# Attention plus token MLP on one core: the opening of the kernel is reordered (zero matmuls first, a long GpSimd memset cut up and put later, a query copy moved into the exponential stream)

## Chip, cores, metric

One core of a Trainium2 chip runs one program. The metric is the device time of one launch in microseconds (us); lower is better. Engines are named as in the profile: PE (TensorE, matmul), PEld (its weight loads), DVE (VectorE), ACT (ScalarE), POOL (GpSimd), SP (SyncE, which issues most DMAs).

## What is computed

The input `x` has 2048 rows (tokens) of 512. The output is `x + A(xn) + B(xn)` with `xn = layernorm(x)`. Cut to what matters:

```python
def A(x):                                   # 32 heads of width 16
    q, k, v = split_heads(x @ wqkv)
    p = softmax(q @ k.T * 16**-0.5)         # 2048 x 2048 for each head
    return merge_heads(p @ v) @ wo

def B(x):                                   # MLP across the tokens
    h = layernorm(x)
    u = gelu(h.T @ w1 + b1)                 # 1376 hidden
    return (u @ w2 + b2).T
```

All inputs and the output are bf16. The softmax is the bulk of it: 32 x 2048 x 2048 exponentials.

## The kernel before

**Tiling.** The tokens are cut in 16 tiles `t` of 128 rows. Queries are taken in 4 blocks of 512 (`qb`) and heads in 8 groups `G` of four, which gives 32 blocks `b`. A block goes through 16 key tiles `kt`; for each, two pairs of score matmuls (`score_mm`, L665: keys as weights, 512 queries moving, one pair for two heads) each fill two PSUM banks, 128x1024. So there are 32 x 16 x 2 = 1024 score pairs. One ACT instruction (`a_exp`, L742) takes the exponential of a whole pair into one of ten `pT` buffers. For some key tiles DVE takes ACT's place with an exponential made of integer and bf16 steps (`d_bits`, `d_chain`, L945 to L985: two reads of 1024 columns out of PSUM and four passes over 2048 columns in SBUF for each key tile). Four PV matmuls (`pv_round`, L766) then add the key tile to bank 6; a tile that went through DVE needs three such rounds.

**Order.** Every engine runs its own queue in order. The queues are written by a planner (`Dispatch`), which simulates the engines with estimated costs (`EST`) and at each simulated moment gives a free engine the ready step of the best priority. Steps become ready by planned times (`at`, `free_at`) and by `prog["p"]`, the number of key tiles scored so far in the plan, to which each score pair adds a half. What the planner writes is a fixed order; at run time only semaphores hold an instruction back. `Sched.add` finds the waits from the keys that each step reads and writes. Two engines that read the same PSUM bank are made to wait for each other as well (the `k[0] == "bank"` lines, L205 to L208). The planner's clock starts at `EST["start"]`.

**The prologue**, before the planned part, is written by hand (`pro_stage`, L601 to L627). `x` is loaded by SP in six DMAs (tiles 0, 1, 2-3, 4-7, 8-11, 12-15), `wqkv` by ACT in six. For a tile, DVE takes statistics (L497, L499), POOL makes the reciprocal deviation with two small instructions (L501, L503), DVE normalises (L512), PE transposes (L523) into a bank that ACT copies out to `xnT` (L518), and PE projects keys (L536), queries (L570) and values (L548) of the first four tiles for the first head group. The key projections of successive tiles use the same bank 6, so each waits until the last one's keys were copied out, on DVE for even tiles and on ACT for odd ones (`kt_tile_evac`). Statistics run to tile 5 here. At the end `qt0_evac` (L575) turns the queries of block 0 and 1, which stand in bank 7 (`EX_BANK`), into `QT`: ACT writes `QT[0]` (L576), DVE writes `QT[2]` (L578), ACT writes an unmasked copy `qst` (L580), and four SP DMAs spread `qst` into `QT[1]` and `QT[3]`, which block 1 needs. All three engine instructions read bank 7.

**The tile loop.** Key tiles 4 to 15 are made while block 0 is being scored (`tile_job`, L1294): for each tile statistics, normalise, transpose, copy, key and value projection, two copies out. DVE does all copies here.

**What POOL does at the start.** `ident` (identity for the transposes), `mhalf`, `zero`, `qmask`, then one memset of `QT[1..7]`, 128 x 3584 (L442), and only then the first L501. `clear_images` (L445) sends the zeroed `QT[4..7]` to a DRAM image, to which later queries are written. `keep_warm` (L1070) inserts pairs of matmuls with zero weights (L1077) where the planner counts too little PE work.

Of the kernel before, what the change touches and what calls it, by code (L numbers as in the profile page):

```python
# [31 lines left out]
NDB = 3  # L32
NPRE = 4
NQS = 4
NW1 = 2
# [13 lines left out]
QSCALE = 0.25 * LOG2E * 128.0  # L49
# [7 lines left out]
EST = dict(  # L57
    start=15.5, pe_switch=0.105, mm512=0.215, mm128=0.065, pe_lat=0.13,
    exp=0.924, exp_lat=1.45, tanh=0.75, act_lat=0.55,
# [15 lines left out]
class Dispatch:  # L75
# [17 lines left out]
    def done(self, *names):  # L93
        t = self.t
        at = self.at
        for n in names:
            if at.get(n, 1e9) > t:
                return False
        return True
# [212 lines left out]
def bass_parallel_sum__softmax_full_mha__mixer_token_mlp__prompt_kernel(  # L312
# [18 lines left out]
    with ExitStack() as es:  # L331
# [19 lines left out]
        qmask = sb("qmask", [128, 2], F32)  # L351
# [3 lines left out]
        QT = sb("QT", [128, 2 * NQS, 512], BF16)  # L355
# [26 lines left out]
        ident = sb("ident", [128, 128], BF16)  # L382
# [26 lines left out]
        def bank(i):  # L409
            return ps[:, i * 512:(i + 1) * 512]  # L410
# [11 lines left out]

        sc.add("pool", lambda e: e.memset(ident[:], 0.0), writes=[("ident",)])
        sc.add("pool", lambda e: e.affine_select(ident[:], ident[:], [[-1, 128]], ALU.not_equal, 1.0,
                                                 base=0, channel_multiplier=1),
               reads=[("ident",)], writes=[("ident",)])
        sc.add("pool", lambda e: e.memset(mhalf[:], -0.5), writes=[("mhalf",)])
        sc.add("pool", lambda e: e.memset(zero[:], 0.0), writes=[("zero",)])
        sc.add("dve", lambda e: e.memset(b1c_bf[:], 0.0), writes=[("b1c",)])
# [4 lines left out]
        sc.add("dve", lambda e: e.memset(v17_main[:, :, 16:17], 1.0), writes=[("Vone",)])  # L434
        sc.add("pool", lambda e: e.memset(qmask[:], 0.0), writes=[("qmask",)])
        for r in range(4):
            sc.add("pool", lambda e, r=r: e.memset(qmask[32 * r:32 * r + 16, r % 2:r % 2 + 1], QSCALE),
                   reads=[("qmask",)], writes=[("qmask",)])
        def qt_at(b, v):
            return 4 * (b // 2 % 2) + 2 * v + b % 2  # L440

        sc.add("pool", lambda e: e.memset(QT[:, 1:2 * NQS, :], 0.0), reads=[("qmask",)],  # L442
               writes=[("QT", q) for q in range(1, 2 * NQS)])

# [130 lines left out]
        def qt0_evac():  # L575
            sc.add("act", lambda e: e.activation(QT[:, 0, :], bank(EX_BANK), ACTF.Identity, scale=qmask[:, 0:1]),  # L576
                   reads=[("bank", EX_BANK), ("qmask",)], writes=[("QT", 0)])
            sc.add("dve", lambda e: e.tensor_scalar(QT[:, 2, :], bank(EX_BANK), qmask[:, 1:2], None, ALU.mult),  # L578
                   reads=[("bank", EX_BANK), ("qmask",)], writes=[("QT", 2)])
            sc.add("act", lambda e: e.activation(qst[:, :], bank(EX_BANK), ACTF.Identity, scale=QSCALE),  # L580
                   reads=[("bank", EX_BANK)], writes=[("qst",)])
            for r in range(4):
                q = 32 * r + 16
                dma("sp", QT[q:q + 16, 1 + 2 * (r % 2), :], qst[q:q + 16, :], reads=[("qst",), ("QT", 1 + 2 * (r % 2))],
                    writes=[("QT1", r)], name="qt_spread")
# [45 lines left out]
        done = dp.done  # L631
        free_at = {("pair", 0): 0.0, ("pair", 1): 0.0, ("pair", 2): None, "b4": 0.0, "b5": 0.0, "ex": 0.0, "pv": 0.0}

# [8 lines left out]
        at[("QT", 0)] = dp.t  # L642
        at[("QT", 1)] = dp.t + 4.0

# [696 lines left out]

        def clear_job():
            def go():
                clear_images()
                dp.use("sp", 2 * EST["sp"])
            yield ("sp", 0.2, lambda: prog["p"] > 2, go)

        dp.spawn(clear_job())
        for t in range(NPRE, NT):
# [150 lines left out]
```

## Time and profile before

| | us |
|---|---|
| median of 3 runs | 796.83 (796.32, 796.83, 798.67) |
| profiled execution, its time | 797.49 |
| its span, first to last instruction | 795.7 |
| ACT busy | 765.9 (96%) |
| PE busy | 723.8 (91%) |
| DVE busy | 714.1 (90%) |
| POOL busy | 73.0 (9%) |
| first exponential starts at | 16.49 |

How to read it: the span is what the profile covers, and 1.8 us of the execution's time lie outside it. Busy shares are averages over the whole span, so the opening, in which ACT, PE and DVE all wait for input, counts little in them. An instruction's row in the timeline gives its start, its duration (or that of several merged, with their number) and in brackets how long its engine was idle before it and what ended that. "Mean ns of one" of an exponential (1131) is longer than the distance between two of them, because they overlap at the ends; 756.5 us of busy time for 816 of them give 0.927 us each.

### The profile page before, as it was taken

How to read it: one execution, taken by the hardware profiler on the slowest of the kernel's cores; microseconds unless marked ns; L12 is line 12 of the kernel's file. 1: busy time of each engine (PE TensorE's matmuls, PEld its weight loads, DVE VectorE, ACT ScalarE, POOL GpSimd, SP SyncE). 2: the span in 40 equal slices, each digit the busy share in tenths (PEclk: the TensorE clock that was granted, in tenths of full speed). 3: DMA queues.
4: the chain of work that ended last, by engine and by line, in shares of the span. 5: the costliest groups of instructions: out<-in, count | busy, mean ns of one | idle time of the engine just before them, and what ended most of it. 6: DMA issues, size and time to landing. Idle time of an engine off the chain costs nothing.

```text
span 795.7 us, 14239 instructions
## 1 busy us (share of the span) xinstructions
PE 723.8 (91%) x5928; PEld 212.0 (27%) x5928; DVE 714.1 (90%) x948; ACT 765.9 (96%) x838; POOL 73.0 (9%) x110
## 2 busy tenths in 40 slices
PE   5999998999999899999899989999999999989885
PEld 3433332322222222222222222222222222222221
DVE  6888988999999799999999989998999999998888
ACT  4999999999999999999999999999999999999994
POOL 5233000000000010000000000000000000000000
PEclk9999999999999999999999999999999999999998
DMA  7402010102112122120302212112131112111001
GB/s 187 110 12 70 16 51 15 38 15 74 45 41 67 39 50 68 41 57 15 96 20 56 72 35 79 36 35 79 42 96 33 50 47 82 45 48 49 16 5 40
DMA packets 85184, 41.28 MB, mean 52 GB/s; under 512 B 61184, under 2 KB 81152, under 8 KB 85120
## 3 DMA queue, kind: packets, MB, share of 16 engines
q1 hardware_dynamic: 81952, 38.80, 18.3%
q10 hardware_dynamic: 3168, 1.57, 0.7%
q8 instruction: 46, 0.75, 0.4%
q14 instruction: 18, 0.15, 0.1%
HBM read 33.69 MB, written 5.37 MB: 49 GB/s over the span
## 4 chain that ended last, share of the span: by engine, by line
ACT 71%; PE 17%; DVE 9%; DMA 1%; issue 1%; POOL 0%; SPq 0%; ACTq 0%; DVEq 0%
ACT pT L742 71%; PE ps L665 7%; PE ps L766 5%; DVE xreg L945 3%; DVE big L979 1%; PE ps L1245 1%; PE ps L1174 1%; DMA xreg<-in_A_x_dram 1%; PE ps L1088 1%; DVE xreg L985 1%; DVE stats L497 0%; PE ps L1077 0%; DVE denb L1435 0%; DVE dmore L972 0%; ACT ga_sb L1203 0%
## 5 line engine op out<-in xcount | busy, mean ns | idle before, releaser
L742 ACT ACTIVATE pT<-ps 128x1024 bf16<-128x1024 f32 x816 | 756.5, 1131 | 8.2 <-PE ps L665 5.9
L665 PE MATMUL ps<-QT,KT 64*128 64x512 bf16 x2048 | 361.1, 385 | 52.7 <-ACT pT L742 30.7
L945 DVE TENSOR_SCALAR xreg<-ps 128x1024 int16<-128x1024 f32 x208 | 254.4, 1223 | 58.0 <-PE ps L665 53.6
L665 PEld LDWEIGHTS ps<-QT,KT 64*128 64x128 bf16 x2048 | 88.8, 93 | 338.9 <-ACT pT L742 219.8
L766 PE MATMUL ps<-pT,V 128*32 128x512 bf16 x1632 | 152.6, 388 | 1.2 <-ACT pT L742 0.9
L979 DVE TENSOR_TENSOR big<-xreg,big 128x2048 bf16<-128x2048 bf16 x104 | 128.2, 1233 | 0.0
L985 DVE TENSOR_SCALAR xreg<-xreg 128x2048 int16<-128x2048 int16 x104 | 73.2, 703 | 1.6
L965 DVE TENSOR_SCALAR big<-xreg 128x2048 int16<-128x2048 int16 x104 | 71.0, 683 | 0.1
L766 PEld LDWEIGHTS ps<-pT,V 128*32 128x32 bf16 x1632 | 37.6, 94 | 91.3 <-issue 84.6
L1245 PE MATMUL ps<-gT,w2blk 128*128 128x512 bf16 (+1 forms) x176 | 54.5, 385 | 0.0
L1174 PE MATMUL ps<-big,w1blk 128*128 128x512 bf16 (+1 forms) x176 | 52.9, 385 | 0.0
L895 POOL TENSOR_TENSOR oTe<-OT,denb 128x512 bf16<-128x512 f32 x15 | 20.7, 1380 | 337.6 <-DVE big L979 107.9
L766 PE MATMUL ps<-big,V 128*32 128x512 bf16 x556 | 48.2, 380 | 0.1
L766 PE MATMUL ps<-xreg,VS 128*32 128x512 bf16 x416 | 40.4, 379 | 0.2 <-DVE xreg L985 0.2
L895 POOL TENSOR_TENSOR oT<-OT,denb 128x512 bf16<-128x512 f32 x12 | 15.9, 1326 | 240.0 <-DMA denb<-den_scr 140.9
L972 DVE TENSOR_SCALAR xreg<-xreg 128x2048 int16<-128x2048 int16 x35 | 25.4, 725 | 0.0
L548 PE MATMUL ps<-wqkv_sb,xnT 128*128 128x128 bf16 x256 | 24.4, 225 | 0.1
L972 DVE TENSOR_SCALAR dmore<-xreg 128x2048 int16<-128x2048 int16 x34 | 24.4, 718 | 0.0
L972 DVE TENSOR_SCALAR big<-xreg 128x2048 int16<-128x2048 int16 x35 | 23.9, 683 | 0.0
L1077 PE MATMUL ps<-xnT,zero 128*128 128x512 bf16 x72 | 21.4, 384 | 0.4 <-ACT KT L518 0.2
L855 DVE COPY OT<-ps 128x512 f32<-128x512 f32 x31 | 21.2, 683 | 0.3 <-PE ps L766 0.2
L503 POOL TENSOR_TENSOR mv<-mv,mhalf 128x1 f32<-128x1 f32 x32 | 18.8, 586 | 2.7
(79 smaller groups left out, 373.0 us busy)
## 6 DMA issues: line engine op xcount, KB each, us to landing
denb<-den_scr SPq DMA_DIRECT2D x31, 256.0 KB
QT<-q_img SPq DMA_DIRECT2D x15, 512.0 KB
w1blk<-in_B_w_dram SPq DMA_DIRECT2D x10, 512.0 KB
w2blk<-in_B_w_dram SPq DMA_DIRECT2D x16, 320.0 KB
w1blk<-in_A_x_dram SPq DMA_DIRECT2D x16, 128.0 KB
out_dram<-osb SPq DMA_DIRECT2D x16, 128.0 KB, 1.7
q_img<-qst SPq DMA_DIRECT2D x30, 64.0 KB
xreg<-in_A_x_dram SPq DMA_DIRECT2D x3, 512.0 KB, 9.1
```

Of the source, the lines that this page charges most:

```text
L548: sc.add("pe", lambda e, ct=ct: e.matmul(bank(bk)[:, 128 * j:128 * (j + 1)], lhsT=xnT[:, ct, 128 * t:128 * (t + 1)], rhs=wqkv_sb[:, ct, 2 ...
L665: sc.add("pe", lambda e: e.matmul(bank(bk), lhsT=KT[64 * (r // 2):64 * (r // 2) + 64, T, 128 * kt:128 * (kt + 1)], rhs=QT[64 * (r // 2):64 ...
L742: sc.add("act", lambda e: e.activation(pT[:, buf, :], ps[:, s_ * 1024:(s_ + 1) * 1024], ACTF.Exp, scale=EXP_SCALE), reads=[("bank", 2 * s_ ...
L766: sc.add("pe", lambda e, r=r, lhs=lhs, rhs=rhs: e.matmul(bank(PV_BANK)[32 * r:32 * r + 32, :], lhsT=lhs, rhs=rhs, start=first, stop=last, ...
L895: sc.add("pool", lambda e: e.tensor_tensor(dst, OT32[:, eb, :], denb[:, :], ALU.mult), reads=[("OT32", eb), ("denb",)], writes=keys, extra ...
L945: sc.add("dve", lambda e: e.tensor_scalar(bv_i[:, i, 1024 * hf:1024 * (hf + 1)], ps[:, s_ * 1024:(s_ + 1) * 1024], EXP_BIAS, 0.0, ALU.add, ...
L965: sc.add("dve", lambda e: e.tensor_scalar(ge_i[:, i, :], bv_i[:, i, :], 0x7F, 0x3F00, ALU.bitwise_and, ALU.bitwise_or), reads=[("bD", i)], ...
L972: sc.add("dve", lambda e: e.tensor_scalar(vp_i(i), bv_i[:, i, :], 0x7F80, None, ALU.bitwise_and), reads=[("bD", i)], writes=[("vD", i)] + ...
L979: sc.add("dve", lambda e: e.tensor_tensor(ge_f[:, i, :], bv_f[:, i, :], ge_f[:, i, :], ALU.mult), reads=[("bD", i), ("eD", i)], writes=[(" ...
L985: sc.add("dve", lambda e: e.tensor_scalar(bv_i[:, i, :], bv_i[:, i, :], LIN_S, None, ALU.add), reads=[("bD", i)], writes=[("bD", i)])
L1174: mms = [lambda st=st: sc.add("pe", lambda e: e.matmul(bank(EX_BANK)[0:m, :], lhsT=w1blk[:, slot, st, 0:m], rhs=h_sb[:, st, :], start=(st ...
L1245: mms.append(lambda ft=ft, m=m: sc.add("pe", lambda e: e.matmul(bank(EX_BANK), lhsT=w2blk[0:m, slot, ft, :], rhs=gT[0:m, ft, :], start=(ft ...
```

## The change

Four edits in the opening, and what they need in the planner.

1. `zero` is now set first on POOL, and `NWARM = 9` matmuls of zeros by zeros, 128x512 into bank 4, stand at the head of PE's queue. `ident` follows `zero`.
2. `qmask` (five small memsets) moves from POOL to DVE, behind the memset of `V17` and ahead of the first statistics.
3. The memset of `QT[1..7]` becomes six memsets of 128x512 (`QT[2]`, which DVE writes in full, is left out), planned by `clear_job` on POOL once `prog["p"]` is above 0.5, 1.0, ... 3.0; `clear_images` follows them.
4. ACT's copy to `qst` and its four DMAs leave the prologue. `qst0_job` plans the copy at the front of ACT's queue once more than two score pairs have been fed, and the DMAs once the copy and the memsets of `QT[1]` and `QT[3]` are planned to be over. Bank 7 counts as taken until then.
5. `EST["start"]` is 12.0 for 15.5.

```diff
+NWARM = 9
-    start=15.5, pe_switch=0.105, mm512=0.215, mm128=0.065, pe_lat=0.13,
+    start=12.0, pe_switch=0.105, mm512=0.215, mm128=0.065, pe_lat=0.13,
...
-        sc.add("pool", lambda e: e.memset(ident[:], 0.0), writes=[("ident",)])
+        sc.add("pool", lambda e: e.memset(zero[:], 0.0), writes=[("zero",)])
+        for _ in range(NWARM):
+            sc.add("pe", lambda e: e.matmul(
+                bank(4), lhsT=zero[:, :], rhs=zero[:, :].unsqueeze(1).broadcast_to([128, 4, 128]), start=True, stop=True),
+                reads=[("zero",)], writes=[("bank", 4)])
+        sc.add("pool", lambda e: e.memset(ident[:], 0.0), reads=[("zero",)], writes=[("ident",)])
...
-        sc.add("pool", lambda e: e.memset(zero[:], 0.0), writes=[("zero",)])
...
-        sc.add("pool", lambda e: e.memset(qmask[:], 0.0), writes=[("qmask",)])
+        sc.add("dve", lambda e: e.memset(qmask[:], 0.0), writes=[("qmask",)])
         for r in range(4):
-            sc.add("pool", lambda e, r=r: e.memset(qmask[32 * r:32 * r + 16, r % 2:r % 2 + 1], QSCALE),
+            sc.add("dve", lambda e, r=r: e.memset(qmask[32 * r:32 * r + 16, r % 2:r % 2 + 1], QSCALE),
...
-        sc.add("pool", lambda e: e.memset(QT[:, 1:2 * NQS, :], 0.0), reads=[("qmask",)],
-               writes=[("QT", q) for q in range(1, 2 * NQS)])
+        def clear_qt(q):
+            sc.add("pool", lambda e: e.memset(QT[:, q, :], 0.0), writes=[("QT", q)])
...
+        def qst0():
             sc.add("act", lambda e: e.activation(qst[:, :], bank(EX_BANK), ACTF.Identity, scale=QSCALE),
                    reads=[("bank", EX_BANK)], writes=[("qst",)])
+
+        def qst0_spread():
             for r in range(4):
...
-        free_at = {("pair", 0): 0.0, ("pair", 1): 0.0, ("pair", 2): None, "b4": 0.0, "b5": 0.0, "ex": 0.0, "pv": 0.0}
+        free_at = {("pair", 0): 0.0, ("pair", 1): 0.0, ("pair", 2): None, "b4": 0.0, "b5": 0.0, "ex": None, "pv": 0.0}
...
-        at[("QT", 1)] = dp.t + 4.0
...
         def clear_job():
+            for k, q in enumerate((1, 3, 4, 5, 6, 7)):
+                def go(q=q):
+                    clear_qt(q)
+                    dp.use("pool", 0.5)
+                    if q == 3:
+                        at[("QT13",)] = dp.t + 0.6
+                yield ("pool", 0.6, lambda k=k: prog["p"] > 0.5 + 0.5 * k, go)
+
             def go():
                 clear_images()
                 dp.use("sp", 2 * EST["sp"])
-            yield ("sp", 0.2, lambda: prog["p"] > 2, go)
-
+            yield ("sp", 0.2, lambda: True, go)
+
+        def qst0_job():
+            def go():
+                qst0()
+                free_at["ex"] = dp.use("act", 0.6) + 0.2
+                at[("qst0",)] = free_at["ex"]
+            yield ("act", 0.0, lambda: a_cur["n"] > 2, go)
+
+            def go():
+                qst0_spread()
+                at[("QT", 1)] = dp.use("sp", 4 * EST["sp"]) + EST["dma"]
+            yield ("sp", 0.1, lambda: done(("qst0",), ("QT13",)), go)
+
+        dp.spawn(qst0_job())
         dp.spawn(clear_job())
```

What the compiled queues show of it: on ACT the `qst` copy now stands behind the second exponential. On POOL the first of the six memsets stands behind L501/L503 of tile 6, four behind those of tile 8, the last behind those of tile 9; none of them waits for a semaphore. The planned order differs from there on in many places: up to the 668th of 1024 score pairs the queues differ, and behind it they are equal but for the buffer numbers of DVE's key tiles. In all there are 814 exponentials on ACT for 816, 105 key tiles on DVE for 104, 76 zero-weight filler matmuls (L1077) for 72, and the nine new ones.

## The prediction

> **What bounds the kernel now.** I read the groups first. ACT's exponentials are busy 756.5 us of a 795.7 us span and were kept waiting 8.2 us in all.
>
> ```profile
> L742 ACT ACTIVATE pT<-ps 128x1024 bf16<-128x1024 f32 x816 | 756.5, 1131 | 8.2 <-PE ps L665 5.9
> ```
>
> So the end is: when the exponentials start (16.49), plus 816 x 0.927 = 756.5, plus some 8 us for the tanh instructions between them, plus the waits, plus the tail. A change in the opening counts only if the stream starts earlier and is not held up again, or if the planner gives ACT fewer exponentials.
>
> Then the chain of work that ended last, cut to the first 11 us (start, length, what):
>
> ```profile
> 2.12 6.91 DMA xreg<-in_A_x_dram
> 9.03 0.02 issue
> 9.05 0.71 DVE stats L497
> ...
> 9.96 0.30 DVE big L512
> 10.26 0.21 DVE KT L519
> ...
> 10.52 0.61 PE ps L536 x4
> ```
>
> The first ten us are set by a transfer: `x` tiles 4 to 7 land at 9.03, DVE's statistics of tile 4 wait for them, and behind these stand the normalise of tile 3 and the copy of tile 0's keys, for which PE waits until 10.52. Nothing ahead of 9.03 on DVE is on the path.
>
> Then the timeline of the opening:
>
> ```profile
> 2.34 3.09 POOL L442 MEMSET QT<- 128x3584 bf16 x1
> ...
> 6.30 0.41 DVE L512 TENSOR_SCALAR big<-xreg,mv 128x512 bf16<-128x512 bf16 x1 [1.32 <-POOL mv L503]
> ...
> 12.34 0.41 DVE L512 TENSOR_SCALAR big<-xreg,mv 128x512 bf16<-128x512 bf16 x1
> ...
> 13.05 0.63 PE L548 MATMUL ps<-wqkv_sb,xnT 128*128 128x128 bf16 x4
> ...
> 14.05 0.39 PE L548 MATMUL ps<-wqkv_sb,xnT 128*128 128x128 bf16 x4
> ...
> 15.84 0.60 ACT L580 ACTIVATE qst<-ps 128x512 bf16<-128x512 f32 x1 [0.90 <-DVE QT L578]
> ```
>
> POOL's memset does hold tile 0's normalise up by 1.32 us. PE is slow until about 13.6 (four matmuls start 0.43 apart) and then twice as fast (0.22). And `qst` waits 0.90 us for DVE while ACT could exponentiate.
>
> Last the tile loop (timeline, 16 to 36 us):
>
> ```profile
> 18.91 0.69 POOL L503 TENSOR_TENSOR mv<-mv,mhalf 128x1 f32<-128x1 f32 x1
> ...
> 28.11 1.94 ACT L742 ACTIVATE pT<-ps 128x1024 bf16<-128x1024 f32 x2 [0.26 <-PE ps L665]
> ...
> 30.34 1.94 ACT L742 ACTIVATE pT<-ps 128x1024 bf16<-128x1024 f32 x2 [0.29 <-PE ps L665]
> ```
>
> From 24 to 35 us a tile takes DVE 2.23 us (28.11 to 30.34), and two exponentials take ACT 1.94: DVE's loop, with POOL's L503 inside it, is the bound here, and ACT waits 0.26 to 0.29 for each tile. An earlier start of ACT alone is lost in that stretch.
>
> **Zero matmuls.** `zero` is ready near 0.95 (the first memset takes 0.20 from 0.73). Four 128-column matmuls on the slow clock start over 0.43, so 512 columns take an estimated 0.43, and nine 3.9 us: over by 4.9. Tile 0's transposes now start at 6.78 and could not before 5.4. Cost: nothing, covered by that gap of PE (if PE starts them only at 3, they push the transposes to 6.9, still ahead of 9.03). Gain: only if the fast clock lasts until 10.52. Between 5.4 and 10.5 PE has six groups of four 128-column matmuls, 6 x 0.22 = 1.3 us in 5. The end of this trace shows what the clock does then (busy by stretch; PEclk is the number behind POOL):
>
> ```profile
> 785.10:788.50 3.40, 1.50 (x9) 0.41 (x5) 3.10 (x7) 0.00 (x0) 0.00 (x0) 1.00 0.00 0
> 788.60:792.00 3.40, 1.20 (x2) 0.18 (x2) 3.33 (x6) 0.00 (x0) 0.00 (x0) 0.50 0.17 60
> ```
>
> Five 512-column matmuls start in the first stretch, 5 x 0.217 = 1.1 us of 3.4 (32%), and then the clock is halved. 1.3 in 5 us (26%) is less. So I take it that the clock drops again before 10.52 and the prologue's PE work, all of it behind 10.52, runs as now: 0. If it stays fast: key projection of tile 3 must still wait for DVE's copy of tile 2's keys, which stands behind the normalise of tile 5 at 12.34 (POOL-bound). Copy at 12.65, matmul at 13.0, queries done at 13.6, so `QT[0]` starts at 13.64 for 14.26: -0.62. The other bound: the clock opens later than 13.6 in some execution, at most +0.3.
> The Trainium skill (TensorE: Matmul & The Clock Gate, Part 1) says that the gate opens after a busy free-running window of about 3.4 us and closes after an idle one; by its rule, with 26% not counted as idle, the term would be -0.62 in place of 0.
>
> **`qmask` on DVE, shorter POOL queue.** Five memsets cost DVE 0.35 (five at b1c's 0.07) to 0.70 us (as on POOL, 1.59 to 2.29); tile 0's normalise still comes earlier than 6.30 (4.04 + 0.9 for L501 and L503 + at most 0.7 = 5.6). All of it lies ahead of the DMA at 9.03: 0. The stall goes, and the transfer is late next.
>
> **`qst` moved.** With `QT[0]` still written 14.26 to 14.95, ACT copies tile 3's keys next (0.27) and the first exponential starts when its scores are there: they start at 15.00, and elsewhere the exponential follows 0.43 later (27.68, 28.11): 15.43 for 16.49. The second follows at 16.36, `qst` at 17.29. The six fillers, now held by ACT's key copy until 16.66, follow the scores at 16.28 and end at 17.68; only then comes the third score pair, so the third exponential starts at 18.11. Now it starts at 16.49 + 2 x 0.947 = 18.38. Gain at that point: -0.27, not -1.06, because `qst` still costs ACT its 0.6 and the fillers hold PE. The DMAs behind `qst` and the memset of `QT[3]` start near 20 for 16.87, with 3.6 us to land; block 1 needs them near 46 us (32 exponentials on). SP's `q_img` and `w1blk` loads slip with them and are not needed before either. 0.
>
> **Six memsets inside the tile loop.** The trace has no 512-column memset on POOL. Floor: 3.09 / 7 = 0.44 us; ceiling: POOL's two-input 128x512 multiply, 1.38 us. I take 0.5, near the floor, since that is the same operation. Queued behind the first piece are L501/L503 of tiles 7 and 8, which end at 19.60 now, and DVE's normalise of tile 8 starts at 19.6: it becomes 0.5 late. DVE has 0.47 us of idle time behind it (0.23 and 0.24, waiting for PE at 20.67 and 22.53), which takes half of that up. The four pieces run from 20.1 to 22.1; tile 9's L501 starts at 22.00 now: 0.1 to 0.2 late. With p for a piece, tile 9's normalise is late by about 5p - 2.4. At p = 0.5 DVE's loop is some 0.25 late at 24 us, and that stays to 34.8, ACT's -0.27 being lost in the longer waits. Sum of the opening: **+0.2** (from -0.5 with the fast clock to +4.5 at p = 1.38).
> The Trainium skill (SBUF — State Buffer, the two separate sides) speaks against this edit: a DVE copy or tensor-scalar of the fast kind and a GpSimd instruction exclude each other for their whole length. In the trace L503 takes 0.57 alone and 0.69 beside L512 and the copy; no row shows a memset there. By the page a piece could wait for a 0.4 us copy, p = 0.9, and the opening would be +2.1.
>
> **The new plan.** ACT has two exponentials less: -2 x 0.927 = **-1.85**. DVE has one key tile more (2 x 1.22 + 0.68 + 0.72 + 1.23 + 0.70 = 5.8 us) and PE two PV rounds and four fillers (2 x 0.22 + 4 x 0.22 = 1.3); DVE idles 82 us and PE 72, so I price both at nothing. If that cover is not where it is needed, exponentials wait for scores. Their listed waits up to 515 us are 5.9 us (1.1 in the tile loop, then 0.5, 2.1, 0.9, 1.3); behind the 668th score pair both plans are equal. The new waits cannot be read from the old trace: between -4.8 (all gone) and +4.8 (doubled). I take 0, and expect about 1.5 either way.
>
> **Sum.** +0.2 - 1.85 = -1.65. The profiled execution took 797.49 (span 795.7), which is 0.66 above the median of the runs, so 795.84 on its footing and **795.2** on that of the runs.
>
> **Rivals.** About 0.3% (2.4 us: below 794.4, above 799.2) is what a measurement can tell from no change.
> 1. The forecast, 0.45: 795.2, own range 793.9 to 796.5.
> 2. Faster: the prologue is shorter than I allow, 0.25. For it: the 1.32 us stall is real, the clock may hold, and the transfer may land earlier in another execution. Against it: 9.03 in the chain. With 1.3 us on DVE's loop and the prologue in place of +0.2, the sum is -3.2: 793.7; with the clock's 0.6 more, 793.1.
> 3. The new plan has fewer waits, 0.12: 3 us less of the 4.8, 792.2.
> 4. Slower: POOL's pieces hold the tile loop. Place: the four pieces ahead of tile 9's L501. It cancels the gain at 5p - 2.4 = 1.9, p = 0.86, and at p = 1.38 gives +4.5 - 1.85 = +2.65: 799.5. For it: four pieces fill the gap of POOL (19.60 to 22.00) almost wholly. Against it: the floor row is the same operation. 0.12.
> 5. The change does not shorten ACT's list in effect: new waits eat the two exponentials, 0.06: 797 to 800.
> Case 1 puts 0.1 of its chance below 794.4, cases 2 and 3 together 0.31; 4 and 5 put 0.09 above 799.2: faster 0.41, same 0.50, slower 0.09. The range takes in case 3 and most of 4.
>
> **What would show it.** First statistics of tile 4 still near 9.0; four 128-column matmuls still 0.43 apart at 11 us; first exponential near 15.4 and third near 18.1; memset pieces of 0.5 us; tile 9's normalise near 23.1; exponentials 814, their idle time near 8. The forecast is wrong if `QT[0]` is written ahead of 13.6, if a piece takes over 0.8 us, or if ACT's waits change by over 2 us.

## The result, and the profile after

| | before | changed |
|---|---|---|
| median (us) | 796.44, 6 runs (795.7 to 798.67) | 802.95, 6 runs (801.64 to 805.07) |
| profiled execution, its span | 797.49, 795.7 | 804.14, 802.3 |
| first, third, 21st, last exponential start at | 16.49, 18.49, 36.62, 783.35 | 15.75, 19.81, 39.22, 789.95 |

The ratio is 1.0083, with a 95% interval of 1.007 to 1.0096: the change makes the kernel slower by 0.8%, or 6.5 us. The forecast was 795.2, and the range 792.0 to 798.8 does not hold the result.

The 21st exponential stands where the tile loop is over, so the last row of the table splits the loss. Up to there the changed kernel is 2.60 us late. From there to the last exponential it takes 750.73 us for 746.73, 4.00 more, although it has two exponentials less.

**The exponentials.** In the groups of the changed kernel (columns: busy us, mean ns of one, then the idle time before them and what ended it):

```profile
L750 ACT ACTIVATE pT<-ps 128x1024 bf16<-128x1024 f32 x814 | 756.3, 1110 | 15.4 <-PE ps L673 11.4 <-PE ps L774 2.0
```

There are 814, as planned, but they are busy for 756.3 us, only 0.2 less than 816 were, and they waited 15.4 us for 8.2. The wait is the result. The stream starts 0.74 earlier (-0.7), is busy 0.2 less, waits 7.2 more, and has the 0.6 us of `qst` inside it: +6.9 of the span's +6.6.

**The opening.** The chain that ended last, in the changed kernel (start, length, what):

```profile
1.65 4.77 DMA xreg<-in_A_x_dram
6.44 0.71 DVE stats L502
...
8.83 0.70 DVE stats L502
9.74 0.30 DVE big L517
10.04 0.21 DVE KT L524
10.30 0.61 PE ps L541 x4
...
17.10 2.34 PE ps L1085 x5
19.44 0.32 PE ps L673 x2
...
20.56 1.84 DVE big L517 x2
```

A transfer still opens the chain (an earlier one, tiles 2 and 3), and tile 4's statistics start at 8.83 where they started at 9.05. Two links are new: the fillers take 2.34 us, and two normalises 1.84. The timeline of the same stretch (start, length, engine and line; idle time before it in brackets):

```profile
0.99 4.02 PE L426 MATMUL ps<-zero 128*128 128x512 bf16 x9 [0.99 <-POOL zero L424]
5.46 0.41 DVE L517 TENSOR_SCALAR big<-xreg,mv 128x512 bf16<-128x512 bf16 x1 [0.20 <-POOL mv L508]
5.93 0.40 PE L528 MATMUL ps<-ident,big 128*128 128x128 bf16 x4 [0.91 <-DVE big L517]
...
15.75 2.08 ACT L750 ACTIVATE pT<-ps 128x1024 bf16<-128x1024 f32 x2 [0.54 <-PE ps L673]
17.10 2.34 PE L1085 MATMUL ps<-xnT,zero 128*128 128x512 bf16 x5 [0.33 <-ACT pT L750]
17.73 0.59 ACT L587 ACTIVATE qst<-ps 128x512 bf16<-128x512 f32 x1
17.83 0.53 POOL L448 MEMSET QT<- 128x512 bf16 x1
...
19.81 3.79 ACT L750 ACTIVATE pT<-ps 128x1024 bf16<-128x1024 f32 x4 [1.49 <-PE ps L673]
20.03 1.92 POOL L448 MEMSET QT<- 128x512 bf16 x4
20.48 1.93 DVE L517 TENSOR_SCALAR big<-xreg,mv 128x512 bf16<-128x512 bf16 x2
```

The nine matmuls end at 5.0 and the first transposes run on the fast clock (four in 0.40 us, 0.61 before). But the six fillers between 16.7 and 19.4 start 0.43 apart again, so the third exponential waits 1.49 us. And two normalises beside four memset pieces take 1.93 us, the first of them 1.61 alone; the same two took 0.89 before. What the clock did is in the busy times by stretch (PEclk is the number behind POOL):

```profile
5.00:9.00 4.00, 1.59 (x23) 1.24 (x23) 3.12 (x10) 1.74 (x4) 2.43 (x7) 1.00 1.03 335
9.00:12.00 3.00, 2.01 (x21) 1.82 (x20) 2.49 (x8) 0.97 (x3) 2.19 (x5) 0.52 1.10 338
12.00:15.00 3.00, 2.75 (x26) 2.48 (x24) 0.80 (x3) 1.52 (x4) 0.08 (x1) 0.50 0.81 171
15.00:19.00 4.00, 3.31 (x9) 1.05 (x10) 3.55 (x9) 2.75 (x5) 1.82 (x5) 0.50 0.30 1
19.00:23.00 4.00, 3.61 (x34) 1.49 (x32) 2.87 (x6) 3.19 (x4) 2.86 (x7) 0.95 0.07 16
```

PE was busy 1.59 us of the four from 5 to 9, and the granted clock then fell to half until past 19. (Ahead of the first opening of the clock the column shows 1.00 although matmuls are slow; there the durations tell it.)

### The profile page after: what moved, and what is told of

It reads as the page before. It is cut to its first block, busy times and chain, and to the rows that moved or that the text cites. A ratio compares the mean times of both kernels' runs of the same rounds, so it can differ in the third digit from the quotient of the medians.

```text
span 802.3 us, 14210 instructions
## 1 busy us (share of the span) xinstructions
PE 715.1 (89%) x5860; PEld 212.7 (27%) x5949; DVE 724.9 (90%) x959; ACT 766.2 (96%) x836; POOL 71.3 (9%) x110
## 4 chain that ended last, share of the span: by engine, by line
ACT 55%; PE 27%; DVE 15%; issue 2%; DMA 1%; POOL 1%; ACTq 0%; SPq 0%
ACT pT L750 54%; PE ps L673 12%; PE ps L774 8%; DVE xreg L953 6%; PE ps L1182 3%; DVE big L987 2%; PE ps L1253 2%; DVE big L973 1%; DVE xreg L993 1%; DVE stats L502 1%; DVE big L517 1%; PE ps L1085 1%; DMA xreg<-in_A_x_dram 1%; ACT ga_sb L1211 1%; DVE xreg L980 1%
## 5 line engine op out<-in xcount | busy, mean ns | idle before, releaser
L750 ACT ACTIVATE pT<-ps 128x1024 bf16<-128x1024 f32 x814 | 756.3, 1110 | 15.4 <-PE ps L673 11.4
L993 DVE TENSOR_SCALAR xreg<-xreg 128x2048 int16<-128x2048 int16 x105 | 76.3, 726 | 1.6
L973 DVE TENSOR_SCALAR big<-xreg 128x2048 int16<-128x2048 int16 x105 | 75.0, 715 | 0.2
L1253 PE MATMUL ps<-gT,w2blk 128*128 128x512 bf16 (+1 forms) x152 | 49.1, 384 | 3.8 <-issue 3.3
L1182 PE MATMUL ps<-big,w1blk 128*128 128x512 bf16 (+1 forms) x157 | 48.5, 385 | 3.0 <-issue 2.9
L980 DVE TENSOR_SCALAR xreg<-xreg 128x2048 int16<-128x2048 int16 x35 | 24.7, 705 | 0.0
L980 DVE TENSOR_SCALAR big<-xreg 128x2048 int16<-128x2048 int16 x35 | 24.1, 688 | 0.0
L1085 PE MATMUL ps<-xnT,zero 128*128 128x512 bf16 x56 | 18.9, 404 | 3.4 <-issue 2.9
L508 POOL TENSOR_TENSOR mv<-mv,mhalf 128x1 f32<-128x1 f32 x32 | 18.6, 582 | 2.7
```

What stands on the lines that cost most here:

```text
L750: sc.add("act", lambda e: e.activation(pT[:, buf, :], ps[:, s_ * 1024:(s_ + 1) * 1024], ACTF.Exp, scale=EXP_SCALE), reads=[("bank", 2 * s_ ...
L973: sc.add("dve", lambda e: e.tensor_scalar(ge_i[:, i, :], bv_i[:, i, :], 0x7F, 0x3F00, ALU.bitwise_and, ALU.bitwise_or), reads=[("bD", i)], ...
L980: sc.add("dve", lambda e: e.tensor_scalar(vp_i(i), bv_i[:, i, :], 0x7F80, None, ALU.bitwise_and), reads=[("bD", i)], writes=[("vD", i)] + ...
L993: sc.add("dve", lambda e: e.tensor_scalar(bv_i[:, i, :], bv_i[:, i, :], LIN_S, None, ALU.add), reads=[("bD", i)], writes=[("bD", i)])
L1085: sc.add("pe", lambda e: e.matmul(bank(PV_BANK), lhsT=zero[:, :], rhs=xnT[:, 0, 0:512], start=first, stop=first), reads=[("zero",)] + [("x ...
L1182: mms = [lambda st=st: sc.add("pe", lambda e: e.matmul(bank(EX_BANK)[0:m, :], lhsT=w1blk[:, slot, st, 0:m], rhs=h_sb[:, st, :], start=(st ...
```

## The experiments

Three theories. **Plan**: the different order of the queues makes the exponentials wait more; the opening has little to do with it. **Clock**: the zero matmuls shift the time at which PE's clock opens, closes and opens again, so that the fillers run slowly. **Pieces**: the memset pieces hold DVE's normalises. Each run was made with the kernel before beside it, and each ratio is to that.

What the expectations call the 20th exponential is the one called the 21st here (36.62 us in the kernel before).

**1. All edits, with the plan of before.** The edits' instructions are put in the queues, but the planner is not told of them (no planned time used, `EST["start"]` as before), so the rest of the order is that of before, with 816 exponentials. Against the changed kernel:

```diff
-    start=12.0, pe_switch=0.105,
+    start=15.5, pe_switch=0.105,
...
-                    dp.use("pool", 0.5)
-                    if q == 3:
-                        at[("QT13",)] = dp.t + 0.6
+                    added.add(q)
...
-                free_at["ex"] = dp.use("act", 0.6) + 0.2
-                at[("qst0",)] = free_at["ex"]
+                added.add("qst")
```

> All edits of the opening as changed, but put into the queues without telling the planner, so that every queue behind the opening is the one of before (816 exponentials). Theory P (two separate costs: the opening is about 2.5 us late at the 20th exponential, and the new plan itself waits some 5 us more between the 20th exponential and the last tanh, of which 1.9 are paid by two exponentials less): +2 to +3.5 us against before. Theory O (one cost: the late opening throws everything behind it out of step, the plan is as good as the old one): +6 us or more, since the opening is the same and there is no saving of two exponentials. Theory N (only the plan costs): within 1 us of before.

797.26 us (11 runs, 796.02 to 799.26), before 796.66; ratio 1.0004 (0.9994 to 1.0014). All four edits of the opening on the old plan cost nothing that can be measured, and gain nothing, as theory N expected.

**2. The old opening, with the new plan.** The reverse: the planner is given the changed numbers, and no instruction of the opening is changed. Against the kernel before:

```diff
-    start=15.5, pe_switch=0.105,
+    start=12.0, pe_switch=0.105,
...
+        def clear_qt(q):
+            pass
```

> The reverse: the opening of before, written into the queues by hand as before, with the planned queues of the changed kernel (814 exponentials, 105 key tiles on DVE). Theory P: +3 to +4.5 us against before (5.4 of new waits less 1.85). Theory O: -1 to -2 us, since two exponentials go and the opening is not late. Theory N: the whole +6.5.

801.43 us (5 runs, 800.83 to 802.65), before 796.66; ratio 1.006 (1.0045 to 1.0076). That is +4.8, a little above theory P and well below theory N: the order of the queues alone gives most of the loss.

**3. Zero matmuls alone.**

```diff
+        for _ in range(NWARM):
+            sc.add("pe", lambda e: e.matmul(bank(4), lhsT=zero[:, :],
+                rhs=zero[:, :].unsqueeze(1).broadcast_to([128, 4, 128]), start=True, stop=True),
+                reads=[("zero",)], writes=[("bank", 4)])
```

> Only the nine zero matmuls at the head of PE (and zero set ahead of ident), all else as before. If they are harmless and useless, as forecast: within 0.7 us of before, first exponential near 16.5, PE slow again from about 10.5 us on. If closing and reopening of the clock costs (in the changed kernel it was slow from 9.1 to 19.4 us, in before it became fast at 13.7): first exponential up to 0.5 later, the six fillers at 0.43 for 0.22 each, third exponential 1 to 2 us later, +1 to +2 us in all in such executions.

796.69 us (11 runs, 795.4 to 797.86); ratio 0.9996 (0.9984 to 1.0008). Nothing either way on the old plan. But in the profiled execution the nine matmuls did not open the clock: groups of four matmuls take 0.60 to 0.63 us until the last one, begun at 13.35, is a little shorter. So this run does not show what an early opening is worth.

**4. Memset pieces (and `qmask` on DVE) alone**, `qst` left in the prologue, old plan.

```diff
-        sc.add("pool", lambda e: e.memset(QT[:, 1:2 * NQS, :], 0.0), ...)
+        def clear_qt(q):
+            sc.add("pool", lambda e: e.memset(QT[:, q, :], 0.0), writes=[("QT", q)])
...
+        dp.spawn(pieces_job())
```

> Only qmask on DVE and the six memset pieces behind POOL's work for tiles 6, 8 and 9, the plan of before, qst in the prologue as before. If the pieces cost what the changed kernel's trace shows (DVE's normalises of tiles 7 and 8 take 1.9 us together for 0.9, beside four pieces of 0.48; tile 4's keys are copied 2.4 us later): DVE's loop +1 to +2 us late and +1 to +2 us in all. If they are hidden as I forecast (0.25 late): within 0.5 us of before.

797.39 us (11 runs, 796.33 to 799.06); ratio 1.0007 (0.9997 to 1.0017). In its profile the 21st exponential starts at 37.82, but the first too is late (17.25), so only 0.44 of the 1.20 us lies between the two. The first is late with the input: tile 2's statistics start at 7.55 here and at 6.63 in the kernel before. Not told from no change.

**5 to 8. What in the planner's input changes the order.** Comparing the queues showed that one number does: with `start` at 12.0 the kernel before gets the changed kernel's planned order, and with 15.5 the changed kernel gets that of before. The effect is not monotonic in it: 10.0, 11.0, 11.5, 11.9, 12.1 and 13.0 give 814 exponentials, as 12.0 does, 12.5, 14.0, 15.0 and 16.0 give 816, as 15.5 does, and 20.0 gives 820 in a third order. The planner adds 0.01 us to a sum at each step and compares with `<=`, so the start decides on which side of a bound a sum of hundredths falls. With 0.000001 us of tolerance in these comparisons and a count of steps in place of the sum, the order is the same for all starts tried from 10 to 20. It is a fourth order.

```diff
-    start=15.5, pe_switch=0.105,
+    start=12.0, pe_switch=0.105,
```

> The kernel before with one number changed: EST start 12.0 for 15.5, nothing else. The planner counts every time from it, so it should be a mere clock origin; yet the planned queues come out as those of the old-opening-new-plan run, with 814 exponentials. Theory R (the plan changes only because sums of 0.01 us steps round differently at another origin, and the plan that happens to come out is worse): about 801.4, +4.8 us. Theory S (the constant is harmless, and the new jobs for ACT, POOL and bank 7 changed the plan): within 0.7 us of before.

801.41 us (5 runs, 800.9 to 802.69); before 796.89; ratio 1.0055 (1.0042 to 1.0067). One number of the planner, and no edit of the opening, gives 4.5 us.

The changed kernel with `start` at 15.5, which gives the order of experiment 1 by another road:

> The changed kernel with its one constant put back: EST start 15.5, all other edits as they are. Theory R: the planned queues are those of before behind the opening, 816 exponentials, about 797.3 (+0.3 to +1 us against before, 5.5 less than the changed kernel). Theory S: 802 to 803.

797.82 us (12 runs, 796.55 to 799.78); ratio 1.0017 (1.0006 to 1.0028). With experiment 1, whose interval overlaps this one: the opening's edits on the old plan cost 0 to 0.3%. Its profile shows another course of the clock (PE's timeline):

```profile
5.92 0.40 PE L528 MATMUL ps<-ident,big 128*128 128x128 bf16 x4 [1.38 <-DVE big L517]
7.62 0.61 PE L528 MATMUL ps<-ident,big 128*128 128x128 bf16 x4 [1.30 <-DVE big L517]
...
10.93 0.39 PE L553 MATMUL ps<-wqkv_sb,xnT 128*128 128x128 bf16 x4
```

Opened, closed again ahead of 7.62, and open for good ahead of 10.93: here `QT[0]` is written at 13.40 and the first exponential starts at 14.58, 1.91 earlier than before. At the 21st 0.43 of that is left (36.19), and the execution took 796.67 us, where the kernel before took 796.89 in the median.

The planner with tolerance:

```diff
-            if at.get(n, 1e9) > t:
+            if at.get(n, 1e9) > t + 1e-6:
...
-            self.t += dt
+            self.t = self.t0 + self.ticks * dt
```

> The kernel before, with a planner that compares times with 1e-6 us of tolerance and counts its steps as whole numbers, so that the plan no longer depends on the clock origin (a plan of its own: 816 exponentials, 70 fillers, different from the old one from the 13th or so matmul group on). If the old plan was a lucky draw among plans of equal worth to the planner: slower than before by 1 to 5 us. If most plans are alike and the changed kernel's was an unlucky one: within 1 us of before.

802.46 us (6 runs, 801.25 to 803.9); ratio 1.0067 (1.0054 to 1.008). The kernel before with `start` at 20.0:

> The kernel before with EST start 20.0: another plan by rounding alone, with 820 exponentials on ACT (four more) and 66 fillers. Four exponentials more are +3.7 us if the waits are equal. If waits decide and not the count: anywhere from 796 to 803. It shows the spread that comes with the plan.

800.56 us (5 runs, 799.88 to 801.46); ratio 1.0043 (1.0031 to 1.0055).

Its profile meets the first expectation: four exponentials more, and no more waiting than the 8.2 us of before.

```profile
L742 ACT ACTIVATE pT<-ps 128x1024 bf16<-128x1024 f32 x820 | 760.1, 1113 | 6.8 <-PE ps L665 4.9
```

So three other orders, all made by rounding alone, are 3.7 to 5.6 us slower than that of before, and not all for one reason: with 20.0 ACT has more to do, with 12.0 it waits more. The profile of the kernel with 12.0 shows where the time lies, for its opening is that of before (first exponential 16.38, 21st 36.90). Its exponentials, over the whole span:

```profile
L742 ACT ACTIVATE pT<-ps 128x1024 bf16<-128x1024 f32 x814 | 756.0, 1116 | 12.3 <-PE ps L665 8.3 <-PE ps L766 2.0
```

They wait 4.1 us more and are busy 0.5 less: +3.6 of the span's +3.8 (799.5 for 795.7). The same group from 36 to 400 us alone, first of the kernel before, then of the one with 12.0:

```profile
L742 ACT ACTIVATE pT<-ps 128x1024 bf16<-128x1024 f32 x386 | 358.0, 1160 | 3.5 <-PE ps L665 1.8 <-PE ps L766 1.3
```

```profile
L742 ACT ACTIVATE pT<-ps 128x1024 bf16<-128x1024 f32 x380 | 353.9, 1118 | 7.2 <-PE ps L665 3.9 <-PE ps L766 2.0
```

Of the 4.1 us, 3.7 lie here; from 400 to 790 they wait 4.1 for 3.5. The busy time is hardly smaller, and a likely reason is that a wait costs more than its listed idle time. An exponential lasts some 1.13 us, of which the next one covers 0.2; the one ahead of a wait is not covered. The waits rose from 22 to 28 in number, and six times 0.2 is an estimated 1.2 of the 1.35 that are missing from two exponentials' 1.85. (In the changed kernel's profile, with 33 waits, 1.65 are missing: 0.15 for each.)

The largest wait of the new order can be read whole. Timeline of the kernel with 12.0:

```profile
156.36 0.69 DVE L855 COPY OT<-ps 128x512 f32<-128x512 f32 x1
...
156.78 0.60 PE L1114 MATMUL ps<-xnT,wqkv_sb 128*128 128x512 bf16 x2
156.97 1.21 DVE L945 TENSOR_SCALAR xreg<-ps 128x1024 int16<-128x1024 f32 x1
...
157.86 0.38 PE L1114 MATMUL ps<-xnT,wqkv_sb 128*128 128x512 bf16 x1 [0.16 <-issue]
...
158.23 0.10 PEld L665 LDWEIGHTS ps<-QT,KT 64*128 64x128 bf16 x2 [0.49 <-DVE xreg L945]
...
158.56 1.26 PE L766 MATMUL ps<-pT,V 128*32 128x512 bf16 x20
159.22 4.69 ACT L742 ACTIVATE pT<-ps 128x1024 bf16<-128x1024 f32 x5 [2.02 <-PE ps L766]
```

A block ends, DVE copies its bank 6 out (156.36 to 157.05), and five key tiles' PV matmuls, 20 in one go, must follow. They are free from 157.05, but PE's queue has four matmuls of a later projection (one is missing from the records) and two score pairs ahead of them, and the second pair waits for DVE, which reads PSUM until 158.18. Until the first of the 20 are done, ACT finds no free `pT` buffer, and idles 2.02 us. The kernel before, on the same kind of work:

```profile
155.18 1.04 PE L1114 MATMUL ps<-xnT,wqkv_sb 128*128 128x512 bf16 x4
...
156.69 0.62 PE L766 MATMUL ps<-pT,V 128*32 128x512 bf16 x8
...
157.56 0.40 PE L766 MATMUL ps<-pT,V 128*32 128x512 bf16 x4
```

Here PV matmuls come in eights and fours between the others, and the exponentials run on from 154.77 for 34.23 us. The wait of 2.02 stands at the same place, with the same length, in the changed kernel's profile (161.36) and in that of experiment 2 (159.89). The old order has one such wait too, of 1.30 us at 286.74, which the new one has not. So from 36 to 400 us waits for PV grew by 0.7 us, and waits for scores by 2.1 (from 7 waits and 1.8 us to 12 and 3.9).

**9 to 12. What the opening adds on the new plan.** The changed kernel without its zero matmuls; with GpSimd's memset whole and early; as it is, once more; and the kernel before with `qst` moved and nothing else.

```diff
-NWARM = 9
+NWARM = 0
```

> The changed kernel without the nine zero matmuls; every queue is otherwise the changed kernel's. Theory A (the pieces hold VectorE's normalises, and that is what the opening costs on the new plan): within 1 us of the changed kernel run beside it, some 802 to 803 us. Theory B (the zero matmuls shift the clock, so that it closes at 9.13 us and the fillers ahead of the third exponential run slowly): 801.0 to 802 us, the time of the new plan behind the old opening, with the third exponential near 18.5 us instead of 19.81 and the fillers at 0.22 us each.

801.65 us (6 runs, 800.95 to 802.31); before 797.01; ratio 1.006 (1.0045 to 1.0076). Timeline:

```profile
15.72 2.08 ACT L750 ACTIVATE pT<-ps 128x1024 bf16<-128x1024 f32 x2 [0.32 <-PE ps L673]
...
16.90 1.24 PE L1085 MATMUL ps<-xnT,zero 128*128 128x512 bf16 x5 [0.16 <-ACT pT L750]
...
18.50 3.81 ACT L750 ACTIVATE pT<-ps 128x1024 bf16<-128x1024 f32 x4 [0.22 <-PE ps L673]
...
20.25 2.05 POOL L448 MEMSET QT<- 128x512 bf16 x4
20.33 0.58 DVE L517 TENSOR_SCALAR big<-xreg,mv 128x512 bf16<-128x512 bf16 x1 [0.46 <-POOL mv L508]
```

Five fillers take 1.24 us for 2.34, and the third exponential starts at 18.50 for 19.81, as the clock theory expected. The normalise beside the four pieces takes 0.58, not 1.6, but it has first waited 0.46 for POOL's L508, which stands behind the first piece.

```diff
-        def clear_qt(q):
-            sc.add("pool", lambda e: e.memset(QT[:, q, :], 0.0), writes=[("QT", q)])
+        clear_qt = lambda q: None
+        sc.add("pool", lambda e: e.memset(QT[:, 1:2 * NQS, :], 0.0), writes=[("QT", q) for q in range(1, 2 * NQS)])
```

> The changed kernel with GpSimd's memset whole again and at its old place in the opening, in the place of the six pieces; the queues of the four other engines are the changed kernel's. Theory A (the pieces hold the normalises): the keys of tile 4 are copied near 20.5 instead of 22.33 us, the 20th exponential comes 1.5 to 2.5 us earlier, and the time falls to 800.5 to 801.5 us. Theory B (the clock): third exponential still near 19.8 us, and 802.5 to 803.5 us.

801.01 us (6 runs, 799.44 to 802.13); ratio 1.005 (1.0034 to 1.0067). Timeline:

```profile
1.71 3.08 POOL L448 MEMSET QT<- 128x3584 bf16 x1
5.67 0.41 DVE L517 TENSOR_SCALAR big<-xreg,mv 128x512 bf16<-128x512 bf16 x1 [0.41 <-POOL mv L508]
...
6.14 0.61 PE L528 MATMUL ps<-ident,big 128*128 128x128 bf16 x4 [1.13 <-DVE big L517]
...
13.15 0.64 PE L553 MATMUL ps<-wqkv_sb,xnT 128*128 128x128 bf16 x4
...
15.45 2.08 ACT L750 ACTIVATE pT<-ps 128x1024 bf16<-128x1024 f32 x2 [0.32 <-PE ps L673]
16.62 1.24 PE L1085 MATMUL ps<-xnT,zero 128*128 128x512 bf16 x5 [0.16 <-ACT pT L750]
...
18.23 9.38 ACT L750 ACTIVATE pT<-ps 128x1024 bf16<-128x1024 f32 x10 [0.21 <-PE ps L673]
```

The time that the pieces theory expected. But in this execution the nine matmuls did not open the clock at all (four matmuls still take 0.61 at 6.14 and 0.64 at 13.15); it opened about when it does without them, and the fillers are fast (1.24), so the profile does not separate the two theories. Its runs do in part. Three show a mean granted clock of 0.995 to 0.996 and took 799.44, 800.03 and 800.82; three show 0.991 to 0.992 and took 801.20, 801.42 and 802.13. The mean of the second three is 1.5 us higher, with the same instructions. The first six runs of the changed kernel go the same way, from 0.989 and 805.07 to 0.997 and 801.64; its second six (below) hardly do. On the old plan it is not so: all edits with `start` 15.5 took 797.36 to 798.65 at 0.991 to 0.992, and 796.55 to 799.46 at 0.996 to 0.997.

The changed kernel again:

> The changed kernel as it is, as the measure for the two runs beside it: 802 to 804 us, 1.007 to 1.0096 of the kernel before. If the plan's share (801.4 us with the old opening) is all there is, 801 to 802 us.

802.63 us (6 runs, 801.73 to 802.8); ratio 1.007 (1.0054 to 1.0086), clock 0.991 to 0.993 in all six. Its profile shows the clock low from 9 to 15 and open again ahead of the fillers:

```profile
9.00:12.00 3.00, 2.60 (x23) 2.33 (x24) 2.93 (x9) 1.35 (x3) 2.38 (x6) 0.50 1.10 341
12.00:15.00 3.00, 3.00 (x31) 3.00 (x29) 1.74 (x6) 1.06 (x4) 1.05 (x3) 0.50 0.87 202
15.00:19.00 4.00, 2.81 (x20) 1.46 (x19) 2.47 (x7) 3.19 (x6) 0.60 (x2) 0.95 0.09 5
```

So the third exponential waits only 0.22 here. The first starts at 16.84, 1.09 later than in the first profile, but not by the clock, which is slow from 9 to 15 in both. The chain of this profile begins with the same transfer as the first one's, and it lands later:

```profile
1.64 6.24 DMA xreg<-in_A_x_dram
7.88 0.02 issue
7.90 0.70 DVE stats L502
```

Tiles 2 and 3 are there at 7.88, and at 6.42 in the first profile. So what the clock cost, 1.28 us at the third exponential, stands in the first profile alone; this one, with the same instructions, does not show it.

> The kernel before with one edit alone: the query copy and its four transfers behind the third exponential instead of ahead of the first, on the plan of before. First exponential 0.2 to 0.4 us earlier in its profile; 796.0 to 796.9 us if nothing else moves (its gain of 0.27 us is within what can be measured). If the copy behind the third exponential holds back the scores that need its copy of the queries, up to 798 us.

796.76 us (12 runs, 795.58 to 798.38); ratio 0.9997 (0.9987 to 1.0007). No difference. The first exponential, expected earlier, starts at 17.21 in its profile: PE's matmuls are slow there up to the last projection at 15.76 (four in 0.63 us).

The starts of the exponentials in these profiles, in us, with the time from the 21st to the last, put the parts side by side:

| kernel | plan | first | third | 21st | 21st to last |
|---|---|---|---|---|---|
| before | old | 16.49 | 18.49 | 36.62 | 746.73 |
| 1, all edits | old | 16.05 | 18.83 | 37.66 | 744.99 |
| 3, zero matmuls | old | 16.86 | 18.86 | 37.00 | 745.37 |
| 4, pieces | old | 17.25 | 19.25 | 37.82 | 745.07 |
| `qst` alone | old | 17.21 | 19.97 | 38.10 | 744.93 |
| all edits, `start` 15.5 | old | 14.58 | 17.36 | 36.19 | 746.41 |
| `start` 12.0 | new | 16.38 | 18.38 | 36.90 | 750.30 |
| 2, old opening | new | 17.10 | 19.10 | 37.65 | 749.55 |
| one memset | new | 15.45 | 18.23 | 36.77 | 749.85 |
| no zero matmuls | new | 15.72 | 18.50 | 37.73 | 750.42 |
| changed again | new | 16.84 | 19.62 | 38.84 | 749.83 |
| changed | new | 15.75 | 19.81 | 39.22 | 750.73 |
| with tolerance | fourth | 17.13 | 19.14 | 37.69 | 751.68 |
| `start` 20.0 | third | 16.23 | 18.23 | 35.15 | 750.51 |

The last column has two groups and nothing between them: 744.9 to 746.7 on the old plan, 749.6 to 751.7 on the others, whatever the opening. The first exponential moves with the input and the clock of the execution. Two with one and the same opening start 0.72 apart (`start` 12.0 and experiment 2; tile 2's statistics start at 7.17 and 7.88 in them), two others 1.47 (experiment 1 and `start` 15.5), so differences of that size in that column are not an edit's.

The distance from the third to the 21st is steadier. Without the pieces it is 18.13 or 18.14 on the old plan and 18.52 to 18.55 on the new. With them it is 18.57 to 18.83 on the old and 19.22 to 19.41 on the new: the pieces hold the tile loop up by 0.4 to 0.9 us in every profile that has them. From the first to the third it is 2.76 to 2.78 in every profile with `qst` moved but that of the changed kernel, where it is 4.06.

No kernel run here beats the one before.

## Why the prediction was wrong

**The step that failed** is "The new waits cannot be read from the old trace: between -4.8 (all gone) and +4.8 (doubled). I take 0, and expect about 1.5 either way." In the kernel with nothing but the new order the listed waits rose by 4.1, near the upper end. The term beside it, -1.85 for two exponentials, shrank to the 0.5 by which the busy time fell, since every added wait also takes an estimated 0.2 us of overlap. The new plan is worth +4.5 us (801.41 for 796.89), not -1.85. That is the mechanism of rival 5, new waits, which had 0.06 of the chance and ended at 800.

**The range contradicted its own bound.** With +4.8 for the waits the sum would have been 800.0 on the runs' footing (795.2 + 4.8), ahead of what the opening adds. The range ended at 798.8. A bound that is written down and left out of the range does no work; and a value in the middle of two bounds is no finding. "Priced at nothing" because DVE and PE idle 82 and 72 us was an average over the span: the wait that was read whole comes from the order in which PE takes PV, projection and score matmuls, and an average does not show it.

**What was overlooked in the diff.** The prediction took the new plan as a result of the edits. It is a result of `start` alone, by rounding. The planner's own clock would have been a warning: from its start to its end it plans 803.5 us for the order of before and 806.4 for the new one. It is no measure, though. For the order with tolerance it plans 801.9, and that one is 5.6 us slower than before (1.0067, 1.0054 to 1.008); for `start` 20.0 it plans 804.2, and 3.7 us were measured.

**The opening, +0.2.** This term was mis-sized too. In the changed kernel's profile it is +2.60. Beside the changed kernel with one memset, whose clock was the old one and which has no pieces, it falls in three: 19.81 for 18.23 at the third exponential, +1.58, of which 1.28 are a longer wait there (1.49 for 0.21) and the rest the later start; and from the third to the 21st 19.41 us for 18.54, +0.87. That other profile meets the forecast times closely (first 15.45 for a forecast 15.43, third 18.23 for 18.11, 21st 0.15 later than before for +0.2), but partly by luck: the +0.2 was for the pieces, which it has not, the 21st is 0.4 late by the new plan itself, and the first moves by a microsecond between executions. By the medians, beside `start` 12.0 at +4.5, the opening adds some 1.1 (802.63 - 797.01 - 4.5) to 2.0 (802.95 - 796.44 - 4.5); only the first set of runs shows it clear of noise (1.007 to 1.0096 beside 1.0042 to 1.0067; the second set's 1.0054 to 1.0086 overlaps).
- *Zero matmuls, hidden.* Right: over at 5.0, transposes at 5.93. *The clock closes again ahead of 10.52.* Right: 0.52 from 9 to 12. But "the prologue's PE work runs as now" was wrong. The clock before opened near 13.6 and stayed open. Of the six profiles with the nine matmuls, two do not have it open any earlier (experiment 3, one memset); in the four others it opens early and closes again, and it is open for good ahead of 10.93 in one (`start` 15.5), past 15 in two (experiment 1, changed again) and past 19 in one (changed). "At most +0.3" for that bound was too small for the last: the fillers alone gave 1.28. Without the nine matmuls the changed kernel took 801.65 for 802.63; the intervals of the two ratios overlap, so what the clock costs the median is likely, not shown.
- The Trainium skill (TensorE: Matmul & The Clock Gate, Part 1) calls the activity window free-running and the cold start different from run to run. The two profiles of the changed kernel agree: same queues, open again past 15 in one and past 19 in the other. It gives an idle window of about 3.4 us as what closes the clock; here it closed with PE busy 1.59 us of 4.00 and never idle for more than 1.38 at a time (from 6.33 to 7.71), so the measurement decides that no idle window is needed.
- *`qmask`, shorter queue: 0.* Right: tile 0's normalise came at 5.46 for 6.30, and the chain still starts with a transfer.
- *A piece takes 0.5 us.* Right: 0.53 alone, 1.92 to 2.05 for four. *The loop is 0.25 late.* Too small: 0.4 to 0.9. That tile 8's normalise becomes 0.5 late was right (it waits 0.46 in the kernel without the zero matmuls); that idle time of DVE takes half of it up was not. And rival 4's mechanism is not the whole: the pieces were not long, DVE's normalises beside them were (0.58 for 0.41, and in the changed kernel's first profile 1.61 for one of them).
- The Trainium skill (SBUF — State Buffer, the two separate sides) says that the one of the two engines that starts first holds the shared ports for its whole instruction. That was the rule that I priced at +2.1 and set aside. The runs agree that either can lose. With the pieces begun at 20.25 and the normalise at 20.33 it took 0.58. In the changed kernel's first profile a normalise begun at 20.48, beside pieces that run from 20.03 to 21.95, took 1.61 us and ended at 22.09, past the last of them. So it did not get its turn ahead of pieces that began after it, which that rule does not say.
- *`qst`: -0.27 at the third exponential.* The forecast's own figure for now, 18.38, is 18.49 in the profile of before. The order of events was right (18.23 with one memset), and alone it gains nothing that can be measured (0.9997, 0.9987 to 1.0007).

**The sum, as it is now:** plan +4.5, measured alone, and the opening +1.1 to +2.0, which is what that leaves of the measured +5.6 (802.63 for 797.01) and +6.5 (802.95 for 796.44).

**What stays open.** Why the order of before is the best of the four. The new order and the one with tolerance wait more (12.3 and 12.6 us for 8.2); the one with `start` 20.0 waits less (6.8) and has four exponentials more. Only one wait of 2 us was read whole; those for scores, 0.2 to 0.5 us each, were not taken apart. How the opening's share splits between clock and pieces in the median: taking out the zero matmuls or the pieces, one at a time, each brings the time to within 0.4 us of the new order alone (801.65 and 801.01 beside 801.41), so the two costs do not simply add. Whether a start that opens the clock early in every execution would gain was not tried; the one profile in which it was open for good ahead of 10.93 had 0.43 us of it left at the 21st exponential.

## What to carry to other kernels

Where a planner writes the queues, a change of its input is a change of the program: compare the queues first, put the edits in the old order and the new order under the old edits, and price both, before crediting an edit with anything. When a term cannot be read from the trace and its bounds are as wide as the whole forecast, let the range reach both ends. Before a late start in one profile is put down to an edit, look when its first input landed. An exponential saved on the bound engine is worth its issue distance only if it adds no wait; count waits as well as their listed time, since each breaks an overlap.

## What the runs showed of the hardware

- Nine matmuls of 512 columns, some 4 us of PE work from 0.99 on, opened PE's clock early in four of six profiles and in two not. Once open it was halved again, in the changed kernel after a stretch with PE busy 1.59 us of 4.00, and stayed so for 3 to 10 us although PE was then busy 2.01 to 3.00 us of every 3. No gain from the nine was measured (0.9996, 0.9984 to 1.0008, on the old plan).
- A DVE normalise of 128x512 (0.41 us) lasted 0.58 where it met a row of four GpSimd memsets at their start, in five profiles, and 1.61 in the one where it began in the midst of the row. The four memsets took 2.05 where the normalise took 0.58 (kernel without the zero matmuls), and 1.92 where it took 1.61.
- The transfer of `x` tiles 2 and 3 landed at 6.42 in one profile of the changed kernel and at 7.88 in the other, and the first exponential moved with it by 1.09 us.
- Differences of 3.7 to 5.6 us of 797 came from orders that differ by rounding in a planner, more than any edit of the opening.
